# One attention-and-MLP block on one core: last q tile moved, a start-up reordered, and two loads and a broadcast rewritten as 128-row copies

## The chip, the cores and the metric

The kernel runs on one core of a Trainium2 chip. The metric is device time in microseconds (us) of one execution. The kernel before takes 828.01 us, the median of three runs (827.72 to 828.8).

## What is computed

```python
x = A_x                                            # 1 x 2048 x 1024, bf16
mod = (silu(c) @ w_mod).reshape(1, 6, 1, 1024)     # sa, ca, ga, sb, cb, gb
h = layernorm(x) * (1 + ca) + sa
q, k, v = split(h @ wqkv)                          # 32 heads of 32
pq, pk = phi(q), phi(k)                            # phi(t) = (t + 1 if t > 0 else exp(t)) + 1e-6
kv = einsum('bhsd,bhse->bhde', pk, v);  z = sum_s pk
o = (pq @ kv) / (pq . z + 1e-6)
x = x + ga * (o @ wo)
h = layernorm(x) * (1 + cb) + sb
x = x + gb * ((silu(h @ w_gate) * (h @ w_up)) @ w_down)
```

## The kernel before

The program writes one list of instructions for each engine by hand, in the order in which the calls stand; semaphore waits are derived from which bytes an instruction reads and writes. Nothing is reordered later, so an instruction that waits holds back all that stand behind it on its engine. All DMAs but one tiny one are issued from SyncE's queue (SP), in order too. A PSUM bank is taken over by another engine only when the last user of the bank is done.

**Start (lines 597 to 660).** Four row tiles of 128 rows are normalised and transposed on TensorE. Tiles 0 and 2 get mean and variance from VectorE (`s0_`, `s2_`: two bn_stats and an aggregation), tiles 1 and 3 from sums on ScalarE (`act_stats`, `ve_sums`). GpSimd raises the variance to -1/2, VectorE applies it (`ln1_xn`, `ln1_xn_sum`), then TensorE transposes 8 blocks (`tile_transposes`). Between them stand filler matmuls on a tile of zeros (`warm`), whose result nobody reads. `mod_sc` makes columns of the scale 1+ca and of the shift sa with one-column matmuls into bank 0; `fin_ca` and `fin_sa` copy them out; `h0_first` scales the transposed tile.

**q of the first 512 rows (`q_phase_chunk0`, lines 773 to 847).** Seven q tiles stand in seven banks and are summed over the 8 blocks `dt` as weights and scales arrive; bank 0 holds the small products. The effect of the shift on q goes through a bias (`bias_mm`, `bias_fin`, `BIASQ`). The eighth q tile comes last, in bank 0. ScalarE evicts each q tile twice (`q_phi`: Exp and Relu), VectorE combines them (`q_min`, `q_add`).

**k of the first 512 rows, then chunks 1 to 3 (lines 849 to 932).** Each `k_group` or `q_group` is 8 matmuls into the bank that `next_bank` gives. `kside` hangs VectorE work behind the k groups of chunk 0, among it the scaling of chunk 1's transposed rows (`th_mod(1, ...)`).

**The middle (lines 934 to 1073).** Since o @ wo is linear in v, the weights are folded: G = x-hat^T pk in 16 `g_group`s of 16 matmuls in five banks, evicted by `g_evac` (ScalarE and VectorE, one group behind); `kvt_mm` and `m_mm` make the folded weight MW from G, WV and WO, a half at a time. `den` makes the denominators on TensorE, VectorE inverts them, the result goes to DRAM (`recip_den`, 32 heads x 2048 rows) and comes back spread over 128 partitions (RB: each head's row on 32 partitions). `scale_pq(hg)` multiplies the phi of q by RB on VectorE; the `wo_part` matmuls then use it. `wo_load` brings wo into WO; `fold_ga` scales WO by ga on VectorE. The order of this stage is the loop of lines 1038 to 1061:

```python
for g in range(16):
    g_group(g)
    while ev < g + 1 - (3 if g < 4 else 2 if g < 6 else 1):
        g_evac(ev); ev += 1
    ...
    if 6 <= g <= 9:  fold_ga(2 * (g - 6)); fold_ga(2 * (g - 6) + 1)
    if g == 10:      kvt_mm(0)
    if 11 <= g < 13: m_mm(0, g - 11, ...)
    if 7 <= g < 15:  scale_pq(g - 7)
```

After the loop stand `g_evac(15)`, four loads of x, six `wo_part` matmuls, `kvt_mm(1)` and the rest of MW. The load `stgx1` reuses the memory of RB, and the loads of x that of the normalised rows.

**The rest.** Projection and residual, the second normalisation, then the gate, up and down matmuls with streamed weights.

Of the kernel before, what the change touches and what calls it, by code (L numbers as in the profile page):

```python
# [5 lines left out]
FP32 = mybir.dt.float32  # L6
# [256 lines left out]
def bass_adaLN_cond__linear_attn_block__swiglu_ffn__prompt_kernel(  # L263
# [22 lines left out]
    with ExitStack() as es:  # L286
# [6 lines left out]
        def T(name, off, shape, dt):  # L293
            n = 1
            for s_ in shape[1:]:
                n *= s_
            assert off % 32 == 0 and off + n * mybir.dt.size(dt) <= ARENA, (name, off, shape)
            return nc.alloc_sbuf_tensor_at(name, shape, dt, offset=base + off)
# [47 lines left out]
        RL = T("rl", 188 * KB, [128, 4, 512], BF16)  # L346
        E1X = T("e1x", 192 * KB, [128, 4, 512], BF16)
        RLX = T("rlx", 196 * KB, [128, 4, 512], BF16)
        ACC = T("acc", 192 * KB, [128, D], FP32)
        MHL = T("mhl", 196 * KB, [128, 2, D], BF16)  # L350
        MHLT = T("mhlt", 192 * KB, [128, 2 * NDT, 128], BF16)
# [105 lines left out]
        def warm(n=1, bank=2):  # L457
            for _ in range(n):
                P.pe("matmul", out=PS[:, bank, :], lhsT=IDENT[:], rhs=E1[:, 0, :], start=True, stop=True)
# [23 lines left out]
        def ln1_xn(st, c0=0, c1=D):  # L483
            P.dve("tensor_scalar", out=XRES[:, st, c0:c1], in0=XRES[:, st, c0:c1],
                  scalar1=MV[:, st, 0:1], scalar2=RSTD[:, st:st + 1], op0=ALU.subtract, op1=ALU.mult)
# [139 lines left out]
                  op0=ALU.add, op1=ALU.add)  # L625
            pool_pow(st)

        warm(13, bank=3)
        act_stats(1)
        act_stats(3)  # L630
        for f in s0_:
# [1 line left out]
        ln1_rstd1(0)  # L633
        msq_neg(1)
        s2_[0]()
        ln1_xn(0)
        tile_transposes(0)
        warm(5, bank=3)
        ve_sums(1)
        s2_[1]()  # L640
        s2_[2]()
        ln1_rstd1(2)
        ln1_xn_sum(1)
        tile_transposes(1)
        warm(1, bank=3)
        msq_neg(3)
        ln1_xn(2, 0, 512)
        ve_sums(3)
        ln1_xn(2, 512, D)
        tile_transposes(2)  # L650
        mod_sc(WCA, 8, range(2))
        ln1_xn_sum(3, 0, 512)
        ln1_xn_sum(3, 512, D)
        fin_ca(0, 2)
        tile_transposes(3)
        mod_sc(WCA, 8, range(2, 4))
        h0_first(0, "dve")
        h0_first(1, "dve")
        raw_copy(4, "dve")
# [43 lines left out]
        def next_bank():  # L703
            i = qk_ctr[0]
            qk_ctr[0] += 1
            return (1, 2, 3, 4, 6, 7, 5, 0)[i % 8] if i < 40 else i % 5 + 1

        def q_group(ch, nt):
            buf, bank = ch % 2, next_bank()
# [39 lines left out]
        def mod_row_b(bank, i, dst):  # L749
# [3 lines left out]
            P.wait_for("sp", [wr])  # L753
            P.dma("mdr%d" % i, dst[:], MDR[i].unsqueeze(0).to_broadcast([128, D]))

        def q_slot(nt):
            return (E1, RL) if nt < 4 else (E1X, RLX)

        def q_phi(nt, bank):
            for buf, fn_ in zip(q_slot(nt), (ACT.Exp, ACT.Relu)):  # L760
                P.act("activation", out=buf[:, nt % 4, :], in_=PS[:, bank, :], func=fn_, bias=BIASQ[:, nt:nt + 1])

        def q_min(nts):
            for nt in nts:
                e = q_slot(nt)[0][:, nt % 4, :]
                P.dve("tensor_scalar", out=e, in0=e, scalar1=1.0, scalar2=1e-6, op0=ALU.min, op1=ALU.add)

        def q_add(nts):
            for nt in nts:
                e, r = q_slot(nt)  # L770
                P.dve("tensor_tensor", out=PQT[:, nt, 0:512], in0=r[:, nt % 4, :], in1=e[:, nt % 4, :], op=ALU.add)

        def q_phase_chunk0():
            qb = [1, 2, 3, 4, 6, 7, 5]
            fin_ca(2, 2)
            for dt in (2, 3):
                h0_first(dt, "dve")
            for nts, dts in ((range(3), (0,)), (range(3), (1,)), ((3, 4, 5, 6), (0, 1))):
                for nt in nts:
                    q_part(nt, qb[nt], dts)  # L780
            for nt in range(7):
                if nt == 4:
                    mod_sc(WCA, 8, range(4, 8))
                    fin_ca(4, 4)
                    for dt in (4, 5):
                        h0_scale_only(dt)
                q_part(nt, qb[nt], (2, 3))
            act_stats(4, (0,))
            for nt in range(7):
                if nt == 6:  # L790
                    mod_sc(WSA, 0, range(6, 8))
                    fin_sa(6, 2)
                    for dt in (6, 7):
                        h0_scale(dt)
                q_part(nt, qb[nt], (4, 5))
            mod_sc(WSA, 0, range(4, 6))
            fin_sa(4, 2, True)
            for dt in (4, 5):
                h0_shift(dt)
            for nt in range(7):  # L800
                if nt == 2:
                    bias_mm((4, 5))
                q_part(nt, qb[nt], (6,))
            for nt in range(7):
                if nt == 1:
                    mod_sc(WSA, 0, range(4), range(4))
                if nt == 3:
                    mod_sc(WSA, 0, range(4), range(4, 8))
                    fin_sa(0, 4, True)
                    ln_ops[1][0]()  # L810
                if nt == 5:
                    bias_mm(range(4))
                    bias_fin()
                q_part(nt, qb[nt], (7,))
            ln_ops[1][1]()
            ln_ops[1][2]()
            ln1_rstd1(5)
            for i, dt in enumerate((4, 5, 0, 1, 2, 3, 6, 7)):
                P.pe("matmul", out=PS[:, 0, :], lhsT=WQK[:, dt, 896:1024], rhs=HT[:, 0, dt, :], start=(i == 0),
                     stop=(i == 7))  # L820
            for dt in range(4):
                h0_shift(dt)
            ln1_xn(5)
            th_dma(5)
            for nt in range(2):
                q_phi(nt, qb[nt])
            act_stats(4, (1,))
            for nt in range(2, 8):
                q_phi(nt, qb[nt] if nt < 7 else 0)
            for f in ln_ops[2]:  # L830
                f()
            act_var(4)
            pool_pow(4)
            for f in ln_ops[3]:
                f()
            ln1_rstd2(6)
            ln1_xn_sum(4)
            th_dma(4)
            q_min((0, 1))
            for st in (6, 7):  # L840
                ln1_xn(st)
                th_dma(st)
            q_add((0, 1))
            for nts in ((2, 3), (4, 5)):
                q_min(nts)
                q_add(nts)
            qk_ctr[0] = 0

        def add(d, k, f):
            d.setdefault(k, []).append(f)  # L850
# [1 line left out]
        kside = {}  # L852
        ln_ops = [ln1_stats_ops(4 + jj) for jj in range(4)]

        for c0 in (0, 256):
            for dt in range(NDT):
                add(kside, 1, lambda dt=dt, c0=c0: th_mod(1, dt, c0, c0 + 256))
        add(kside, 1, lambda: q_min((6, 7)))
        add(kside, 1, lambda: q_add((6, 7)))
        for jj, k in ((0, 3), (1, 4)):  # L860
            add(kside, k, lambda jj=jj: act_stats(10 + jj))
        q_phase_chunk0()
        for st in range(12, 16):
# [68 lines left out]
        phi_flush()  # L932

        def wo_load(f):
            outs = [WO[32 * g:32 * g + 32, 4 * f:4 * f + 4, :] for g in range(4)]

            def fn(e, outs=outs, f=f):
                return [e.dma_start(out=o_, in_=wov[f, g]) for g, o_ in enumerate(outs)]

            P.add("sp", fn, reads=[], writes=outs, lane="wo%d" % f, ninc=4, tag="wo")  # L940

        G_BANKS = [0] + [next_bank() for _ in range(4)]

# [26 lines left out]
        def den():  # L970
            for hg in range(NHG):
                for ch in range(NCH):
                    P.pe("matmul", out=PS[32 * ch:32 * ch + 32, 7, :], lhsT=ZSEL[:, hg * 32:hg * 32 + 32],
                         rhs=PQT[:, hg, ch * 512:(ch + 1) * 512], start=(hg == 0), stop=(hg == NHG - 1),
                         skip_group_check=True)
            P.dve("tensor_scalar", out=DEN[:], in0=PS[:, 7, :], scalar1=1e-6, scalar2=None, op0=ALU.add)
            P.dve("reciprocal", out=RCP[:], in_=DEN[:])
            P.dve("tensor_copy", out=RCB[:], in_=RCP[:])
            wr = [P.dma("rdr%d" % ch, RDR[:, ch * 512:(ch + 1) * 512], RCB[32 * ch:32 * ch + 32, :])
                  for ch in range(NCH)]  # L980
            P.wait_for("sp", wr)
            for gh in range(2):
                outs = [RB[32 * hh:32 * hh + 32, 4 * gh:4 * gh + 4, :] for hh in range(4)]
                ins = [RDR.rearrange("(g x) s -> x g s", x=4)[hh, 4 * gh:4 * gh + 4].unsqueeze(0).to_broadcast([32, 4, S])
                       for hh in range(4)]

                def fn(e, outs=outs, ins=ins):
                    return [e.dma_start(out=o_, in_=i_) for o_, i_ in zip(outs, ins)]

                P.add("sp", fn, reads=[], writes=outs, lane="rb%d" % gh, ninc=4, tag="rb")  # L990

        def scale_pq(hg):
            P.dve("tensor_tensor", out=PQT[:, hg, :], in0=PQT[:, hg, :], in1=RB[:, hg, :], op=ALU.mult)
# [254 lines left out]
```

## Time and profile before

| what | us |
|---|---|
| median of three runs | 828.01 |
| the profiled execution, its own time | 827.71 |
| span of its instructions | 826.0 |
| VectorE busy in the span | 312.2 (38%) |
| ScalarE busy | 197.0 (24%) |
| GpSimd busy | 41.0 (5%) |
| one 128x512 matmul, start to start | 0.216 |
| one g_group (16 matmuls) | 3.45 |

A matmul's own record is longer (0.379 us) than its pitch of 0.216 us, since matmuls overlap in the array. Times inside the execution count from the first instruction. The 1.7 us between span and own time lie around the program. The stages by the clock of the trace: start to 12 us, q of the first rows to 29 us, k and q of all rows to 126 us, the middle to about 192 us, the projection to about 240 us, the MLP to the end.

### The profile page before, as it was taken

Reading aid. Unit: us, or ns where it says so; the run is one execution under the profiler, and the core shown is the slowest. Engines: PE = TensorE matmul, PEld = TensorE weight load, DVE = VectorE, ACT = ScalarE, POOL = GpSimd, SP = SyncE. Lnnn points to the kernel's source line nnn. Section 1 sums busy time; section 2 is a strip of 40 time slices with the busy share of each in tenths; the row PEclk is TensorE's granted clock in tenths of the full one; section 3 lists DMA queues with packets and bytes.
Section 4 is the critical chain, followed back from the end, with each engine's and each line's share of the span. In section 5 each row is a group of like instructions: output and inputs, shape, how many; then the busy total and the mean of one; then the engine's idle time right before and its main releaser. Section 6 shows DMA issues by size and latency. Waiting matters only on the chain.

```text
span 826.0 us, 10436 instructions
## 1 busy us (share of the span) xinstructions
PE 816.3 (99%) x4243; PEld 375.9 (46%) x4322; DVE 312.2 (38%) x672; ACT 197.0 (24%) x338; POOL 41.0 (5%) x58
## 2 busy tenths in 40 slices
PE   8999999999999999999999999999999999999998
PEld 4544444444444444444444444444444444444444
DVE  5798988477945521111221112122111111221111
ACT  4758642123341111011111101111110111111011
POOL 1110000000130000020000003000000300000000
DMA  9969756865698995600455570045557004553000
GB/s 316 297 139 223 167 159 149 181 175 211 149 253 245 296 249 153 166 26 26 136 151 151 153 174 25 23 131 153 151 152 182 27 19 126 151 152 88 0 26 26
DMA packets 199392, 119.32 MB, mean 144 GB/s; under 512 B 58024, under 2 KB 183088, under 8 KB 199344
## 3 DMA queue, kind: packets, MB, share of 16 engines
q1 hardware_dynamic: 199328, 118.65, 53.8%
q8 instruction: 34, 0.56, 0.3%
q14 instruction: 14, 0.11, 0.0%
q10 hardware_dynamic: 16, 0.00, 0.0%
HBM read 100.67 MB, written 4.33 MB: 127 GB/s over the span
## 4 chain that ended last, share of the span: by engine, by line
PE 98%; issue 1%; DMA 0%; DVE 0%; POOL 0%; SPq 0%
PE ps L176 98%; DMA xres<-in_A_x_dram 0%; POOL rstd L176 0%; DVE xres L176 0%; DVE stats L176 0%; SPq L176 0%; DVE ht L176 0%; DVE ve L176 0%; DVE mv L176 0%; DVE modcol L176 0%
## 5 line engine op out<-in xcount | busy, mean ns | idle before, releaser
L176 PE MATMUL ps<-h2t,gug 128*128 128x512 bf16 x878 | 210.1, 379 | 0.9
L176 PE MATMUL ps<-h2t,guu 128*128 128x512 bf16 x878 | 209.9, 379 | 0.9
L176 DVE TENSOR_TENSOR at<-sg,ps 128x512 bf16<-128x512 bf16 x112 | 77.0, 687 | 282.8 <-PE ps L176 270.6
L176 ACT ACTIVATE sg<-ps 128x512 bf16<-128x512 f32 x112 | 66.9, 597 | 309.7 <-PE ps L176 298.3
L176 PEld LDWEIGHTS ps<-h2t,guu 128*128 128x128 bf16 x896 | 87.7, 98 | 105.7
L176 PEld LDWEIGHTS ps<-h2t,gug 128*128 128x128 bf16 x896 | 87.6, 98 | 105.5
L176 PE MATMUL ps<-wd_a,at 128*128 128x512 bf16 (+1 forms) x502 | 111.9, 377 | 0.5
L176 PE MATMUL ps<-ht,wqk 128*128 128x512 bf16 x499 | 110.7, 379 | 0.9 <-DVE ht L176 0.2
L176 PE MATMUL ps<-wd_b,at 128*128 128x512 bf16 (+1 forms) x377 | 84.6, 377 | 0.4
L176 PEld LDWEIGHTS ps<-wd_a,at 128*128 128x128 bf16 x512 | 50.1, 98 | 59.6
L176 DVE TENSOR_TENSOR ut<-att,gb_b 128x512 bf16<-128x512 bf16 (+1 forms) x32 | 13.6, 426 | 167.5 <-ACT att L176 167.5
L176 PEld LDWEIGHTS ps<-ht,wqk 128*128 128x128 bf16 x512 | 49.2, 98 | 58.9 <-DVE ht L176 1.0
L176 ACT ACTIVATE att<-ps 128x512 bf16<-128x512 f32 (+1 forms) x32 | 17.4, 591 | 182.1 <-PE ps L176 182.1
L176 PEld LDWEIGHTS ps<-wd_b,at 128*128 128x128 bf16 x384 | 37.6, 98 | 44.7
L176 PE MATMUL ps<-pk,xres 128*128 128x512 bf16 x250 | 55.4, 379 | 0.6 <-issue 0.5
L176 PE MATMUL ps<-mw,pqt 128*128 128x512 bf16 x249 | 55.4, 379 | 0.5 <-issue 0.2
L176 POOL TENSOR_SCALAR h2t<-h2t,modcol 128x512 bf16<-128x512 bf16 x32 | 26.5, 846 | 383.0 <-DMA h2t<-xn 383.0
L176 ACT ACTIVATE e<-ps 128x512 bf16<-128x512 f32 x56 | 33.3, 611 | 31.8 <-PE ps L176 15.8
L176 ACT ACTIVATE junk<-xres 128x1024 bf16<-128x1024 bf16 x26 | 27.6, 1063 | 45.9 <-DVE xres L176 34.2
L176 PEld LDWEIGHTS ps<-mw,pqt 128*128 128x128 bf16 x256 | 24.8, 98 | 30.0 <-issue 0.5
L176 PEld LDWEIGHTS ps<-pk,xres 128*128 128x128 bf16 x256 | 24.6, 98 | 30.1 <-issue 1.3
L176 DVE SCALAR_TENSOR_TENSOR xres<-ps,xres 128x512 bf16<-128x512 f32 x32 | 21.5, 688 | 11.6 <-PE ps L176 11.3
(111 smaller groups left out, 337.8 us busy)
## 6 DMA issues: line engine op xcount, KB each, us to landing
gug<-in_B_w_gate_dram SPq DMA_DIRECT2D x56, 512.0 KB, 4.0
guu<-in_B_w_up_dram SPq DMA_DIRECT2D x56, 512.0 KB, 5.3
xres<-in_A_x_dram SPq DMA_DIRECT2D x20, 256.0 KB, 4.4
rb<-recip_den SPq DMA_DIRECT2D x8, 512.0 KB, 11.7
stgx<-in_w_mod_dram SPq DMA_DIRECT2D x2, 2048.0 KB, 9.3
wd_a<-in_B_w_down_dram SPq DMA_DIRECT2D x4, 1024.0 KB, 7.7
out_dram<-xres SPq DMA_DIRECT2D x31, 128.0 KB, 1.7
xres<-in_A_x_dram SPq DMA_DIRECT2D x3, 1024.0 KB, 6.5
```

The lines of the kernel that those rows point to most:

```text
L176: return getattr(e, method)(**kw)
```

## The change

- **Start:** 14 instead of 13 fillers ahead of the first transposes, then 1 and 2 in place of 5 and 1. Tile 2's second bn_stats, tile 1's variance and tile 2's aggregation stand ahead of tile 0's normalisation on VectorE. The scale columns are made 3 and 1 tiles at a time in place of 2 and 2.
- **q of the first rows:** the first q tile is copied out raw (`QRAW`, one more ScalarE instruction), and the eighth q tile takes its bank instead of bank 0. The eighth tile's matmuls stand around the shift and bias products. Both passes of tile 4's statistics stand together, the q tiles are finished in the order 1 to 7, then 0, and the bank order of the k groups follows.
- **Side work of chunk 0's k:** th_mod of blocks 4 to 7 goes at full width (12 instructions in place of 16), the last four q tiles are combined behind the fourth k group, and two statistics move one group later.
- **DMAs of the middle:** `wo_load`, the write of the reciprocals and their broadcast RB get another form; sizes and count of loads (8 of 256 KB, 8 of 512 KB) stay, the write is one of 128 KB in place of four of 32 KB. RB now has a semaphore for each of its 8 blocks in place of one for 4 blocks.

In the built program the leading counts of the access patterns are, DRAM side first:

| copy | before | after |
|---|---|---|
| wo | 32 x 4 x 1024 to 32 partitions x 4 x 1024 | 4 x 32 x 1024 to 128 partitions x 1024 |
| recip_den, written | 32 x 512 from 32 partitions | 4 x 32 x 512 from 128 partitions |
| recip_den, read into RB | 32 (step 0) x 4 x 2048 to 32 partitions x 4 x 2048 | 4 x 32 (step 0) x 2048 to 128 partitions x 2048 |

```diff
-        warm(13, bank=3)
+        warm(14, bank=3)
...
         s2_[0]()
+        s2_[1]()
+        ve_sums(1)
+        s2_[2]()
+        ln1_rstd1(2)
         ln1_xn(0)
         tile_transposes(0)
-        warm(5, bank=3)
-        ve_sums(1)
-        s2_[1]()
-        s2_[2]()
-        ln1_rstd1(2)
+        warm(1, bank=3)
         ln1_xn_sum(1)
         tile_transposes(1)
-        warm(1, bank=3)
+        warm(2, bank=3)
...
-        mod_sc(WCA, 8, range(2))
+        mod_sc(WCA, 8, range(3))
...
-        fin_ca(0, 2)
+        fin_ca(0, 3)
         tile_transposes(3)
-        mod_sc(WCA, 8, range(2, 4))
+        mod_sc(WCA, 8, range(3, 4))
...
             for nt in range(7):
-                if nt == 1:
+                q_part(nt, qb[nt], (7,))
+                if nt == 0:
+                    P.act("activation", out=QRAW[:], in_=PS[:, qb[0], :], func=ACT.Copy)
+                    act_stats(4)
+            for i, dt in enumerate(range(NDT)):
+                if i == 1:
                     mod_sc(WSA, 0, range(4), range(4))
-                if nt == 3:
+                if i == 3:
                     mod_sc(WSA, 0, range(4), range(4, 8))
+                    ln_ops[1][0]()
                     fin_sa(0, 4, True)
...
+                P.pe("matmul", out=PS[:, qb[0], :], lhsT=WQK[:, dt, 896:1024], rhs=HT[:, 0, dt, :], start=(i == 0),
+                     stop=(i == 7))
...
-        for c0 in (0, 256):
-            for dt in range(NDT):
-                add(kside, 1, lambda dt=dt, c0=c0: th_mod(1, dt, c0, c0 + 256))
-        add(kside, 1, lambda: q_min((6, 7)))
-        add(kside, 1, lambda: q_add((6, 7)))
+        for dt, c0, c1 in ([(dt, 0, 256) for dt in range(4)] + [(dt, 256, 512) for dt in range(4)]
+                           + [(dt, 0, 512) for dt in range(4, 8)]):
+            add(kside, 1, lambda dt=dt, c0=c0, c1=c1: th_mod(1, dt, c0, c1))
+        for i in (4, 6):
+            add(kside, 3, lambda i=i: q_pair(i))
...
         def wo_load(f):
-            outs = [WO[32 * g:32 * g + 32, 4 * f:4 * f + 4, :] for g in range(4)]
+            outs = [WO[:, 4 * f + h, :] for h in range(4)]
...
-                return [e.dma_start(out=o_, in_=wov[f, g]) for g, o_ in enumerate(outs)]
+                return [e.dma_start(out=o_, in_=wov[f, :, :, h, :]) for h, o_ in enumerate(outs)]
...
-            wr = [P.dma("rdr%d" % ch, RDR[:, ch * 512:(ch + 1) * 512], RCB[32 * ch:32 * ch + 32, :])
-                  for ch in range(NCH)]
-            P.wait_for("sp", wr)
-            for gh in range(2):
-                outs = [RB[32 * hh:32 * hh + 32, 4 * gh:4 * gh + 4, :] for hh in range(4)]
...
+            wr = P.dma("rdr", RDR.rearrange("h (c s) -> c h s", c=NCH), RCB[:])
+            P.wait_for("sp", [wr])
+            for hg in range(NHG):
+                rb_ = RB[:, hg, :]
+                rows = RDR[4 * hg:4 * hg + 4, :].unsqueeze(1).to_broadcast([4, 32, S])
```

More of the change, by code (lines that the diff above doesn't have):

```diff
@@ L348, in bass_adaLN_cond__linear_attn_block__swiglu_ffn__prompt_kernel @@
         RLX = T("rlx", 196 * KB, [128, 4, 512], BF16)
+        QRAW = T("qraw", 202 * KB, [128, 512], FP32)
         ACC = T("acc", 192 * KB, [128, D], FP32)
@@ L705, in next_bank @@
             qk_ctr[0] += 1
-            return (1, 2, 3, 4, 6, 7, 5, 0)[i % 8] if i < 40 else i % 5 + 1
+            if i < 24:
+                return (0, 2, 3, 4, 6, 7, 5, 1)[i % 8]
+            if i < 40:
+                return (0, 2, 3, 4, 6, 1, 7, 5, 0, 2, 3, 1, 4, 6, 7, 5)[i - 24]
+            return i % 5 + 1
         def q_group(ch, nt):
@@ L754, in mod_row_b, with q_phi @@
             P.dma("mdr%d" % i, dst[:], MDR[i].unsqueeze(0).to_broadcast([128, D]))
+        QORD = (1, 2, 3, 4, 5, 6, 7, 0)
         def q_slot(nt):
-            return (E1, RL) if nt < 4 else (E1X, RLX)
-        def q_phi(nt, bank):
+            i = QORD.index(nt)
+            bufs = (E1, RL) if i < 4 else (E1X, RLX)
+            return [t[:, i % 4, :] for t in bufs]
+        def q_phi(nt, src):
             for buf, fn_ in zip(q_slot(nt), (ACT.Exp, ACT.Relu)):
-                P.act("activation", out=buf[:, nt % 4, :], in_=PS[:, bank, :], func=fn_, bias=BIASQ[:, nt:nt + 1])
+                P.act("activation", out=buf, in_=src, func=fn_, bias=BIASQ[:, nt:nt + 1])
         def q_min(nts):
             for nt in nts:
-                e = q_slot(nt)[0][:, nt % 4, :]
+                e = q_slot(nt)[0]
                 P.dve("tensor_scalar", out=e, in0=e, scalar1=1.0, scalar2=1e-6, op0=ALU.min, op1=ALU.add)
@@ L770, in q_add, with q_pair @@
                 e, r = q_slot(nt)
-                P.dve("tensor_tensor", out=PQT[:, nt, 0:512], in0=r[:, nt % 4, :], in1=e[:, nt % 4, :], op=ALU.add)
+                P.dve("tensor_tensor", out=PQT[:, nt, 0:512], in0=r, in1=e, op=ALU.add)
+        def q_pair(i):
+            q_min(QORD[i:i + 2])
+            q_add(QORD[i:i + 2])
         def q_phase_chunk0():
             qb = [1, 2, 3, 4, 6, 7, 5]
-            fin_ca(2, 2)
+            fin_ca(3, 1)
             for dt in (2, 3):
@@ L787, in q_phase_chunk0 @@
                 q_part(nt, qb[nt], (2, 3))
-            act_stats(4, (0,))
             for nt in range(7):
@@ L804, in q_phase_chunk0 @@
             for nt in range(7):
-                if nt == 1:
+                q_part(nt, qb[nt], (7,))
[4 more added lines that the diff above has]
+                if i == 1:
                     mod_sc(WSA, 0, range(4), range(4))
-                if nt == 3:
+                if i == 3:
                     mod_sc(WSA, 0, range(4), range(4, 8))
+                    ln_ops[1][0]()
                     fin_sa(0, 4, True)
-                    ln_ops[1][0]()
-                if nt == 5:
+                    ln_ops[1][1]()
+                    act_var(4)
+                    pool_pow(4)
+                if i == 5:
                     bias_mm(range(4))
                     bias_fin()
-                q_part(nt, qb[nt], (7,))
-            ln_ops[1][1]()
+                P.pe("matmul", out=PS[:, qb[0], :], lhsT=WQK[:, dt, 896:1024], rhs=HT[:, 0, dt, :], start=(i == 0),
+                     stop=(i == 7))
             ln_ops[1][2]()
             ln1_rstd1(5)
-            for i, dt in enumerate((4, 5, 0, 1, 2, 3, 6, 7)):
-                P.pe("matmul", out=PS[:, 0, :], lhsT=WQK[:, dt, 896:1024], rhs=HT[:, 0, dt, :], start=(i == 0),
-                     stop=(i == 7))
             for dt in range(4):
                 h0_shift(dt)
+            ln1_xn_sum(4)
+            th_dma(4)
             ln1_xn(5)
             th_dma(5)
[L825 to L829, printed above, removed]
+            for nt in QORD:
+                q_phi(nt, QRAW[:] if nt == 0 else PS[:, qb[nt % 7], :])
             for f in ln_ops[2]:
                 f()
-            act_var(4)
-            pool_pow(4)
             for f in ln_ops[3]:
@@ L836, in q_phase_chunk0 @@
             ln1_rstd2(6)
-            ln1_xn_sum(4)
-            th_dma(4)
-            q_min((0, 1))
+            q_min(QORD[0:2])
             for st in (6, 7):
@@ L842, in q_phase_chunk0 @@
                 th_dma(st)
[L843 to L846, printed above, removed]
+            q_add(QORD[0:2])
+            q_pair(2)
             qk_ctr[0] = 0
@@ L853, in bass_adaLN_cond__linear_attn_block__swiglu_ffn__prompt_kernel @@
         ln_ops = [ln1_stats_ops(4 + jj) for jj in range(4)]
-        for c0 in (0, 256):
-            for dt in range(NDT):
-                add(kside, 1, lambda dt=dt, c0=c0: th_mod(1, dt, c0, c0 + 256))
-        add(kside, 1, lambda: q_min((6, 7)))
-        add(kside, 1, lambda: q_add((6, 7)))
-        for jj, k in ((0, 3), (1, 4)):
+        for dt, c0, c1 in ([(dt, 0, 256) for dt in range(4)] + [(dt, 256, 512) for dt in range(4)]
[3 more added lines that the diff above has]
+            add(kside, 3, lambda i=i: q_pair(i))
+        for jj, k in ((0, 4), (1, 5)):
             add(kside, k, lambda jj=jj: act_stats(10 + jj))
@@ L934, in wo_load @@
         def wo_load(f):
-            outs = [WO[32 * g:32 * g + 32, 4 * f:4 * f + 4, :] for g in range(4)]
+            outs = [WO[:, 4 * f + h, :] for h in range(4)]
             def fn(e, outs=outs, f=f):
-                return [e.dma_start(out=o_, in_=wov[f, g]) for g, o_ in enumerate(outs)]
-            P.add("sp", fn, reads=[], writes=outs, lane="wo%d" % f, ninc=4, tag="wo")
+                return [e.dma_start(out=o_, in_=wov[f, :, :, h, :]) for h, o_ in enumerate(outs)]
+            P.add("sp", fn, reads=[], writes=[WO[:, 4 * f:4 * f + 4, :]], lane="wo%d" % f, ninc=4, tag="wo")
         G_BANKS = [0] + [next_bank() for _ in range(4)]
@@ L978, in den, with fn @@
             P.dve("tensor_copy", out=RCB[:], in_=RCP[:])
-            wr = [P.dma("rdr%d" % ch, RDR[:, ch * 512:(ch + 1) * 512], RCB[32 * ch:32 * ch + 32, :])
-                  for ch in range(NCH)]
-            P.wait_for("sp", wr)
-            for gh in range(2):
-                outs = [RB[32 * hh:32 * hh + 32, 4 * gh:4 * gh + 4, :] for hh in range(4)]
[L984 to L990, printed above, removed]
+            wr = P.dma("rdr", RDR.rearrange("h (c s) -> c h s", c=NCH), RCB[:])
[3 more added lines that the diff above has]
+                rows = RDR[4 * hg:4 * hg + 4, :].unsqueeze(1).to_broadcast([4, 32, S])
+                def fn(e, rb_=rb_, rows=rows):
+                    return [e.dma_start(out=rb_, in_=rows)]
+                P.add("sp", fn, reads=[], writes=[RB[:, hg, :]], lane="rb%d" % hg, tag="rb")
         def scale_pq(hg):
```

## The prediction

> **What bounds the kernel now.** The busy row comes first, then what PE waited for (columns: us, times, mean us), then the middle cut into windows.
>
> ```profile
> PE 816.3 (99%) x4243; PEld 375.9 (46%) x4322; DVE 312.2 (38%) x672; ACT 197.0 (24%) x338; POOL 41.0 (5%) x58
> ```
>
> ```profile
> PE ps L176 <- DMA cs<-in_c_dram: 2.2, 1, 2.2
> PE ps L176 <- issue: 0.6, 4, 0.2
> PE ps L176 <- DVE e L176: 0.2, 1, 0.2
> PE ps L176 <- DVE ht L176: 0.2, 1, 0.2
> ```
>
> PE sets the time. The 2.2 us lie ahead of the first filler, the 0.2 on `e` is the filler's zeros. All other waits of PE sum to 0.8 us, and between dense matmuls I find only four gaps of the reordered parts (22.4, 26.1, 44.4 and 46.4 us: 0.09, 0.06, 0.04, 0.13). Whatever the edits of the first 60 us do, they can win about half a us; what they can lose is open. So the question is what new wait PE meets, and the place to look is where transfers change form.
>
> ```profile
> 137.00:147.00 10.00, 9.95 (x47) 4.55 (x47) 7.53 (x8) 4.47 (x7) 0.00 (x0) 1.00 1.00 226
> 151.00:161.00 10.00, 9.95 (x47) 4.58 (x47) 2.13 (x4) 0.72 (x1) 0.00 (x0) 1.00 0.99 218
> 161.00:170.00 9.00, 8.84 (x165) 4.53 (x164) 8.72 (x12) 1.45 (x2) 0.00 (x0) 1.00 1.00 205
> 173.00:177.00 4.00, 3.84 (x33) 1.62 (x32) 3.10 (x6) 1.72 (x4) 0.00 (x0) 1.00 1.05 400
> ```
>
> Columns: length, busy of PE, PEld, DVE, ACT, POOL, granted clock, busy DMA engines (1.00 is all 16), GB/s. Row one is wo, rows two and three RB: all 16 engines busy, at 226, 218 and 205 GB/s, 12.8 to 14.1 per engine. Row four is x, loaded as 128 rows: 400, or 23.8 per engine (16.8 by the share).
>
> ```profile
> 161.28 1.22 DVE L176 TENSOR_TENSOR pqt<-pqt,rb 128x2048 bf16<-128x2048 bf16 x1 [6.65 <-DMA rb<-recip_den]
> 166.39 1.28 PE L176 MATMUL ps<-g,wv 128*32 128x32 bf16 x128
> 187.26 1.19 PE L176 MATMUL ps<-g,wv 128*32 128x32 bf16 x128
> ```
>
> These are `scale_pq(0)`, `kvt_mm(0)` and `kvt_mm(1)` (start, length, in brackets the idle time before). VectorE already stands 6.65 us in order behind the first half of RB (landed 161.25, the second 170.98), and PE does not feel it yet.
>
> **The change, part by part.** *Start.* Dense work now begins near 11.8 us. The chain to it is x landed 6.61, tile 3's sums 8.97, variance 9.30, GpSimd 9.59 to 10.24, normalised 10.27, transposes 10.74, `h0_first` 11.14. None of it is removed; tile 2's 1.2 us of bn_stats go ahead of tile 0's normalisation, which takes VectorE work from the later path and delays transposes(0) from 6.98 to about 8.0, with filler 14 ending near 7.13 (start plus 14 at the pitches shown by the first 13: eight at 0.427, then 0.216). The clock was warm after eight fillers, each 0.211 longer than later ones; if the 0.85 us of idleness cooled it again, 7 x 0.211 = 1.5 us are lost. I take a gain of 0.2 (bounds: 0.3 won, 1.5 lost): no wait of that length after warming stands in this trace. Scale columns 3+1 instead of 2+2 are the same 64 small matmuls.
>
> *q and k of the first rows.* Added: one ScalarE copy of 128x512, priced by the like eviction at 0.61; ScalarE is busy 3.17 of 15.2 us from 12 to 27.2, and six matmuls (1.3 us) pass before its bank is written again. Without cover it costs at most 0.6. The eighth tile's 8 matmuls are moved, not added. What changes is the gaps above: 0.2 won of 0.32. The four fewer th_mod instructions and later q adds ease VectorE at 44 to 60 us (15.75 of 16 busy). Were that to pile up instead, I bound it by two half-width instructions, 1 us. Start and q together: -0.4 (bounds -0.6 to +3.1, both losses and an uncovered copy).
>
> *wo, reciprocals, RB.* Bytes are equal: 2.097 MB, 0.131 MB, 4.194 MB. The SP queue issues them in the old order, the write with one instruction for four, the RB copies eight as before; nothing is moved past another queue. What differs is the leading count, now 4 in DRAM against 128 in SBUF. In this trace the count tells how many engines serve a copy: the semaphores of the copies with 8 leading rows (c and the two modulation rows) rise in 9 steps, those with 32 or 128 rows in 16 steps. All have one count on both sides, so 4 against 128 is not shown. I take the smaller to divide the copy: four engines of 16. The other bound is all 16, priced below.
>
> [...]
>
> The price per engine has two ends: 12.8 to 14.1 (32-row rows above, all engines into a quarter of the partitions) and 23.8 (128 rows). The destination is now 128 rows of 2 or 4 KB, as in the row of x, so I take 23.8. No row shows a lone engine.
>
> - wo: 524,288 B for each of four engines / 23.8 = 22.0 us. At 226 GB/s wo took 9.3 and ended at 147.9 (last issue 138.3, longest landing 9.6), so it began at 138.6, and now ends at 160.6. Its first half lands near 149.6, when `fold_ga(0)` wants it (149.9).
> - Reciprocals: 32,768 B, 1.4 us, behind wo on the same four engines: 162.0 (before: 149.2).
> - RB: before, its first half landed 12.0 us after the issue at 149.3, of which 2.097 MB at 218 GB/s are 9.6; 2.4 are start-up. Now 131,072 B each, 5.5 us: the first lands at 162.0 + 2.4 + 5.5 = 169.9, the eighth at 164.4 + 44.1 = 208.5.
>
> What is late next: `scale_pq(g-7)` stands in VectorE's list after each group, and it holds back `g_evac` behind it, the copy of KVT, and so PE. `kvt_mm(0)` needs the eviction of group 7, behind `scale_pq(0)`: it starts late once RB's first block lands after about 164. Group 14 needs a bank evicted behind `scale_pq(4)`. `kvt_mm(1)` needs the eviction of group 15, behind `scale_pq(7)`: that is the last wait, and the earlier ones lie inside it. After RB's last block come 1.21 (scale) and two evictions, 2.6 us with what stands between, then the 0.44 from eviction to `kvt_mm(1)` (186.82 to 187.26): 211.5, against 187.26. **+24.2 us.** The loads of x queue behind RB on the same engines: `stgx1` needs `scale_pq(3)` and took 9 us, the next are wanted later in the projection, which moves too; I count nothing (bound: 2 us).
>
> Before `kvt_mm(1)`, PE has stood for several us; the clock warms again, as in the first fillers: +1.5.
>
> **Sum.** Span 826.0 - 0.4 + 24.2 + 1.5 = 851.3. Around the span lay 1.7 (own time 827.71), and the median of the runs is 0.3 above it: +2.0, so **853 us**.
>
> **Rivals.**
> - *Half rate.* [...] By 13.8 per engine wo takes 38.0 (176.6), the write 2.4 (179.0), RB 2.4 + 8 x 9.5 (257.4), `kvt_mm(1)` comes at 257.4 + 3.0 = 260.4, +73.2; 902 us. With 12.8 per engine wo takes 41.0 and RB 81.9, 911. For: every copy here that leaves most partitions out ran at that rate with all engines busy. [...]
>
> [...]
>
> - *All 16 engines (not slower).* The copies are divided by their 128 SBUF rows, or by descriptors. RB then lands by 400 GB/s in 10.5 us, earlier than before, which PE does not feel: the 6.65 us of VectorE go, PE was at 9.95 of 10. The time is 828.0 - 0.4 = 827.6. It decides wherever RB's first block lands before 164 and one follows each 3.45 us (a group). For: the loop's order still places one scaling per group from group 7 on, fitting blocks that land apart. Against: the 9 steps.
> - *The start cools the clock*, with 16 engines: 828.0 + 1.5 - 0.2 = 829.3. For: 0.85 us without a matmul; against: clock rows show 1.00 throughout once warm.
>
> **How the numbers follow.** Four engines at full rate 0.36 (own range 850 to 874: 1.606 MB per engine take 67.5 us at 23.8, 64.2 at 400/16 = 25, 85.4 at 18.8, midway to the half rate; the 3.1 of the start on top), half rate 0.30, all 16 engines 0.28 (0.03 of it with a gain over 0.2%), start or VectorE slower 0.06 (half over 0.2%). About 0.2%, 1.7 us, is what a measurement tells from no change. Slower: 0.36 + 0.30 + 0.03 = 0.69; same 0.25 + 0.03 = 0.28; faster 0.03. The range reaches from 827 (16 engines) to 906, midway between the half rate's 902 and 911.
>
> **What would show it.** Right: DMA share near 0.25 at about 95 GB/s from 139 to 208, eight waits of VectorE on `rb` of some us each, PE waiting on `g` before `kvt_mm(0)`, in group 14 and before `kvt_mm(1)` at about 211, where the granted clock falls. At 55 GB/s to 257 the half rate is right. Start: transposes(0) at about 8.0, dense work near 11.6, one `qraw` copy on ScalarE, and no gaps at 44 to 47. Wrong: RB's first block by 160 and no wait of PE, a share of 1.00 in that stage, or a loss that lies ahead of 130 us.

## The result, and the profile after

The changed kernel takes 855.65 us (median of five, 854.07 to 857.12), the kernel before 828.01 us in the same comparison: a ratio of 1.033, 95% interval 1.0313 to 1.0347. The execution in the profile took 854.07, its span is 852.3, 26.3 us more than before.

First the busy row of the page, then the chain that ended last, by engine.

```profile
PE 821.3 (96%) x4241; PEld 377.2 (44%) x4320; DVE 312.3 (37%) x668; ACT 197.8 (23%) x339; POOL 40.8 (5%) x58
...
PE 82%; DMA 7%; SPq 3%; DVE 3%; ACT 3%; issue 1%; POOL 0%; ACTq 0%; DVEq 0%
```

The chain was 98% PE before and now has 7% of DMA in it. What PE waited for (us, times, longest):

```profile
PE ps L176 <- DVE g L176: 16.0, 2, 13.7
PE ps L176 <- DVE kvt L176: 4.0, 1, 4.0
PE ps L176 <- DMA cs<-in_c_dram: 2.8, 1, 2.8
PE ps L176 <- issue: 1.0, 5, 0.3
PE ps L176 <- DVE ht L176: 0.6, 2, 0.4
PE ps L176 <- ACT ht L176: 0.4, 1, 0.4
```

Twenty us are new waits for VectorE's evictions. They name VectorE, but VectorE was itself waiting. Its timeline has the eight `scale_pq`; six of them are shown, without the other work (start, length, in brackets the idle time before):

```profile
167.59 1.23 DVE L176 TENSOR_TENSOR pqt<-pqt,rb 128x2048 bf16<-128x2048 bf16 x1 [12.43 <-DMA rb<-recip_den]
...
172.61 1.23 DVE L176 TENSOR_TENSOR pqt<-pqt,rb 128x2048 bf16<-128x2048 bf16 x1 [1.93 <-DMA rb<-recip_den]
...
187.69 1.23 DVE L176 TENSOR_TENSOR pqt<-pqt,rb 128x2048 bf16<-128x2048 bf16 x1 [1.92 <-DMA rb<-recip_den]
...
193.67 1.22 DVE L176 TENSOR_TENSOR pqt<-pqt,rb 128x2048 bf16<-128x2048 bf16 x1 [2.89 <-DMA rb<-recip_den]
...
201.94 1.23 DVE L176 TENSOR_TENSOR pqt<-pqt,rb 128x2048 bf16<-128x2048 bf16 x1 [6.39 <-DMA rb<-recip_den]
...
208.47 1.23 DVE L176 TENSOR_TENSOR pqt<-pqt,rb 128x2048 bf16<-128x2048 bf16 x1 [4.65 <-DMA rb<-recip_den]
```

All eight end a wait for RB, 35.1 us in all; before, the one wait of this kind was 6.65. Up to the fifth, a block comes each 5.03 us (in the trace's semaphores they land at 167.56 to 187.67); the last three take 6.0, 8.3 and 6.5 us, and the eighth lands at 208.45. PE's timeline shows where that is felt, with `kvt_mm(0)`, the first `m_mm`, the first projection matmuls and `kvt_mm(1)`:

```profile
169.62 0.96 PE L176 MATMUL ps<-g,wv 128*32 128x32 bf16 x100 [2.33 <-DVE g L176]
...
179.81 0.44 PE L176 MATMUL ps<-wo,kvt 32*32 32x512 bf16 x16 [3.99 <-DVE kvt L176]
...
210.42 1.03 PE L176 MATMUL ps<-mw,pqt 128*128 128x512 bf16 x2 [13.70 <-DVE g L176]
...
213.09 1.23 PE L176 MATMUL ps<-g,wv 128*32 128x32 bf16 x128
```

The windows of this stage (length, busy of PE, PEld, DVE, ACT, POOL, granted clock, DMA share, GB/s):

```profile
150.00:160.00 10.00, 9.95 (x47) 4.56 (x47) 3.66 (x6) 1.44 (x2) 0.00 (x0) 1.00 0.25 97
...
170.00:180.00 10.00, 5.86 (x98) 2.52 (x90) 5.85 (x9) 1.02 (x2) 0.00 (x0) 0.83 0.26 106
180.00:190.00 10.00, 9.83 (x65) 3.80 (x51) 5.39 (x7) 3.71 (x7) 0.00 (x0) 0.83 0.26 106
190.00:200.00 10.00, 6.72 (x32) 2.84 (x29) 2.67 (x4) 1.12 (x2) 0.00 (x0) 1.00 0.97 219
200.00:210.00 10.00, 0.00 (x0) 0.00 (x0) 3.41 (x4) 0.72 (x1) 0.00 (x0) 0.58 0.59 169
210.00:220.00 10.00, 8.98 (x183) 4.01 (x187) 4.54 (x10) 2.17 (x4) 0.00 (x0) 0.73 0.14 54
```

A share of 0.25 is four engines of 16, and 106 GB/s by 0.26 x 16 engines are 25.5 GB/s for each; before, RB ran at a share of 0.99 to 1.00 with 218 and 205 GB/s. The semaphores say the same in the trace: each of the eight RB copies is counted up in 5 steps, one lump at the issue and four engines. At 190 the share jumps to 0.97 and RB gets slower: there the load `stgx1`, issued at 184.65, runs on the other twelve. The last column but two is the second finding: the granted clock is below 1.00 after each of these waits of PE (0.83, 0.83 and 0.73), and within the longest.

### The profile page after: what moved, and what is told of

It reads as the page before. It is cut to its first block, busy times and chain, and to the rows that moved or that the text cites. A ratio compares the mean times of both kernels' runs of the same rounds, so it can differ in the third digit from the quotient of the medians.

```text
span 852.3 us, 10425 instructions
## 1 busy us (share of the span) xinstructions
PE 821.3 (96%) x4241; PEld 377.2 (44%) x4320; DVE 312.3 (37%) x668; ACT 197.8 (23%) x339; POOL 40.8 (5%) x58
## 4 chain that ended last, share of the span: by engine, by line
PE 82%; DMA 7%; SPq 3%; DVE 3%; ACT 3%; issue 1%; POOL 0%; ACTq 0%; DVEq 0%
PE ps L176 82%; DMA rb<-recip_den 4%; SPq L176 2%; DMA recip_den<-rcb 2%; SPq L996 2%; DMA xres<-in_A_x_dram 1%; DVE pkt L176 1%; ACT e L176 1%; ACT rl L176 1%; ACT junk L176 1%; DVE ht L176 0%; DMA ht<-xres 0%; DVE e L176 0%; DVE acc L176 0%; ACT ht L176 0%
## 5 line engine op out<-in xcount | busy, mean ns | idle before, releaser
L176 PE MATMUL ps<-mw,pqt 128*128 128x512 bf16 x249 | 56.9, 386 | 14.5 <-DVE g L176 13.7
L176 PE MATMUL ps<-pk,xres 128*128 128x512 bf16 x250 | 58.8, 395 | 0.6 <-issue 0.5
```

The source lines that it names most:

```text
L176: return getattr(e, method)(**kw)
```

## The experiments

Each experiment gives its median and, in brackets, its ratio to the kernel before with the 95% interval. The kernel before, measured beside them, took 828.00 us for the first two sections and the first try on the gaps, 827.89 for the three sections between, and 828.15 for the last two runs.

### Taking the copies back

```diff
-            outs = [WO[:, 4 * f + h, :] for h in range(4)]
+            outs = [WO[32 * g:32 * g + 32, 4 * f:4 * f + 4, :] for g in range(4)]
...
-            wr = P.dma("rdr", RDR.rearrange("h (c s) -> c h s", c=NCH), RCB[:])
+            wr = [P.dma("rdr%d" % ch, RDR[:, ch * 512:(ch + 1) * 512], RCB[32 * ch:32 * ch + 32, :])
+                  for ch in range(NCH)]
...
-                rows = RDR[4 * hg:4 * hg + 4, :].unsqueeze(1).to_broadcast([4, 32, S])
+                outs = [RB[32 * hh:32 * hh + 32, 4 * gh:4 * gh + 4, :] for hh in range(4)]
...
```

> The changed kernel with the three copies (wo, reciprocals, RB) in the form of before; all else as changed. Theory (the copies with a leading count of 4 make the whole loss): the loss of 27.6 us is gone, all copies of the stage show 16 increments of their semaphores per copy, kvt_mm(1) comes within 1 us of 187.3, and the time is 827.5 to 829.0. Within it, the gap that the changed kernel shows at 71.5 us (0.8 us, q or k matmuls that wait for the shifted rows of chunk 2) stays, so that the time is rather 828.3 than 827.6. Rival (the reordering of the first 60 us carries part of the loss): 830 or more.

Measured: 828.34 us against 828.00 (1.0005, 0.9996 to 1.0013); RB arrives early enough again, and PE has no wait over 0.3 us after 12 us. `kvt_mm(1)` comes 0.55 us later than in the kernel before:

```profile
187.81 1.20 PE L176 MATMUL ps<-g,wv 128*32 128x32 bf16 x128
```

The three copies make the whole loss, as far as it stands out from the noise. The small gaps stay, as was said: behind the matmuls at 71.7 and 72.6 the next one starts 0.48 and 0.26 us later than the pitch of 0.216.

### Each copy by itself

RB alone, in the kernel before:

```diff
-            for gh in range(2):
-                outs = [RB[32 * hh:32 * hh + 32, 4 * gh:4 * gh + 4, :] for hh in range(4)]
...
+            for hg in range(NHG):
+                rb_ = RB[:, hg, :]
+                rows = RDR[4 * hg:4 * hg + 4, :].unsqueeze(1).to_broadcast([4, 32, S])
...
```

> The kernel before with RB's read alone in the changed form (8 copies of 4 rows by 32, a semaphore each); wo, the write of the reciprocals and the start as before. Theory (4 engines, 26 GB/s each as the changed kernel showed): reciprocals in DRAM at 149.2 as before, first block 7.5 us later at 156.7, then one each 5.05 us until the load of stgx1 collides with the last three; the eighth at 192 without and 198 with that collision. kvt_mm(0) is on time (no wait at 166), group 14 and the bank for the first projection matmuls wait; kvt_mm(1) at 197 to 202.5; time 838 to 844. Rival (wo is what makes RB late, RB's own copies are hidden): 829 or less.

Measured: 844.02 us (1.0191, 1.0177 to 1.0205), at the upper edge of 838 to 844. `kvt_mm(0)` is on time (166.87, no wait), RB's blocks are used at 157.87, 162.90, 167.91 and so on each 5.0 us, then the last three at 6.2, 8.1 and 6.4 us: the slow end of the changed kernel again. PE has one wait:

```profile
200.43 2.74 PE L176 MATMUL ps<-mw,pqt 128*128 128x512 bf16 x6 [13.49 <-DVE g L176]
```

And wo alone, in the kernel before:

```diff
-            outs = [WO[32 * g:32 * g + 32, 4 * f:4 * f + 4, :] for g in range(4)]
+            outs = [WO[:, 4 * f + h, :] for h in range(4)]
...
```

> The kernel before with the loads of wo alone in the changed form. Theory (4 engines): wo's second half lands near 158.8 instead of 147.8; the write of the reciprocals goes through all 16 engines, but its share on those four stands behind wo, so that it ends near 159.5 and RB's first half lands near 171.5 (before 161.25), the second near 181. kvt_mm(0) waits some 7 us at 166.5, one cold restart of the clock of 1.7 us follows, and nothing else waits long: time 836 to 839. Rival (wo's lateness costs nothing by itself, since fold_ga has slack): 828 to 829.

Measured: 838.04 us (1.0119, 1.0103 to 1.0134). The loads of wo end at 159.5, the write of the reciprocals, in its old form over 16 engines, at 160.2; the semaphore of each of its four copies shows twelve engines done at 152 to 154 and four at 158 to 160. RB's first half lands at 172.06, 10.8 us later than before. VectorE waits for it, and PE has one long wait, at `kvt_mm(0)`:

```profile
172.08 1.23 DVE L176 TENSOR_TENSOR pqt<-pqt,rb 128x2048 bf16<-128x2048 bf16 x1 [17.43 <-DMA rb<-recip_den]
...
174.12 0.99 PE L176 MATMUL ps<-g,wv 128*32 128x32 bf16 x100 [7.34 <-DVE g L176]
```

This is how a transfer that nobody waits for costs time: `fold_ga` had slack, what stood behind wo on its four engines had none. The two parts, 16.0 and 10.0 us, sum to 26.0 of the 27.6. That they nearly add is chance in part, as we read it: wo's lateness stalls PE at 166, RB's slow arrival at 187. The new form of the write was not tried alone; behind wo it ended at 160.1 in the new form (the changed kernel) and at 160.2 in the old (here).

### Is it the leading count that sets the engines?

```diff
-                rb_ = RB[:, hg, :]
-                rows = RDR[4 * hg:4 * hg + 4, :].unsqueeze(1).to_broadcast([4, 32, S])
+                rb_ = [RB[64 * i:64 * i + 64, hg, :] for i in range(2)]
+                rows = [RDR[4 * hg + 2 * i:4 * hg + 2 * i + 2, :].unsqueeze(1).to_broadcast([2, 32, S]) for i in range(2)]
...
```

> The changed kernel with each block of RB read by two copies of 2 rows by 32 into 64 partitions, in place of one of 4 rows by 32 into 128; bytes, rows and bytes per row as in the changed kernel. Theory (the smaller leading count sets the number of engines, and copies of the same count use the same engines): each copy shows 3 increments of its semaphore, two engines carry everything, a block takes 10.1 us, the DMA share of the stage is near 0.13, the eighth block lands at 243 to 249, kvt_mm(1) comes near 250, time 890 to 898. Rival (the engines are given by rows, one for each 32, or two copies take different engines): four engines again, a block each 5 us, time 853 to 858.

Measured: 893.27 us (1.079, 1.0769 to 1.0812). Each copy is counted up in three steps, both copies of a block use the same two engines one after the other (a block's halves land 5.0 us apart), and a block takes 10.0 us. A window of that kernel in which RB runs alone, columns as above:

```profile
175.00:185.00 10.00, 5.90 (x115) 2.82 (x116) 3.09 (x5) 0.73 (x2) 0.00 (x0) 0.78 0.13 54
```

0.13 of 16 are two engines; 54 GB/s are 26 for each. The bytes, the rows in all and the length of a row are unchanged; each copy has half the rows. What halved is the leading count, and with it the engines. The rival (engines by the place of a group of 32 rows, or two copies on different engines) would have stayed at four. One engine for each 32 rows of a copy would also give two, but the load `stgx1` has 128 rows and is counted in 16 steps. In none of the changed copies is the smaller count on the SBUF side, so whether the smaller count decides or the one on the DRAM side is not told apart.

### Why RB's last blocks were slow

`rbs` are the eight copies of RB; the loads now wait until the last of them has landed.

```diff
...
-            if g == 10:
-                P.dma("stgx1", STGX[0][:], wmv[:, :, 3072:4096])
         g_evac(15)
+        P.wait_for("sp", rbs[7:])
         for st in range(4):
             P.dma("xr%d" % st, XRES[:, st, :], xv[:, st, :])
+        P.dma("stgx1", STGX[0][:], wmv[:, :, 3072:4096])
```

> The changed kernel with the loads of x and of stgx1 held back until RB's last block has landed (in the changed kernel stgx1 is issued at 184.65 and the blocks of RB that land after 190 take 6.0, 8.3 and 6.5 us in place of 5.05). Theory (those loads, on the 12 engines that are free, slow the four that carry RB): all blocks at 5.05, the eighth at 203 instead of 208.4, kvt_mm(1) 5.5 us earlier, time 849.5 to 852 unless x is then late. Rival (the last blocks are slow for another reason, such as a full queue): the eighth block at 208 again, time 855 or more.

Measured: 849.73 us (1.026, 1.0243 to 1.0277), 5.9 below the changed kernel. In its profile the last three blocks keep the distance of the others, 5.0 us each:

```profile
192.01 1.22 DVE L176 TENSOR_TENSOR pqt<-pqt,rb 128x2048 bf16<-128x2048 bf16 x1 [1.91 <-DMA rb<-recip_den]
...
197.00 1.22 DVE L176 TENSOR_TENSOR pqt<-pqt,rb 128x2048 bf16<-128x2048 bf16 x1 [1.91 <-DMA rb<-recip_den]
...
202.00 1.23 DVE L176 TENSOR_TENSOR pqt<-pqt,rb 128x2048 bf16<-128x2048 bf16 x1 [3.11 <-DMA rb<-recip_den]
...
206.97 1.23 DVE L176 TENSOR_TENSOR pqt<-pqt,rb 128x2048 bf16<-128x2048 bf16 x1 [3.09 <-DMA rb<-recip_den]
```

So a load on twelve idle engines is not free for the four that carry RB: beside it their 4 KB packets took 284 ns in the mean between 192 and 200, where it was 160 between 165 and 190. The loads slowed as well: 2 KB packets took 150 ns between 192 and 200, and 85 between 173 and 177 in the kernel before, where `stgx1` ran alone. What makes each slower beside the other was not tried. (This execution, at 852.88 the longest of four, stands 2.6 us late from its first stage on, for a reason told below, and RB's first block 4.5 us; only distances are read from it.)

### What a cold clock costs

```diff
+        for _ in range(62):
+            P.pe("matmul", out=PS[:, 7, :], lhsT=IDENT[:], rhs=WV[:, 0, 0:512], start=True, stop=True)
         wo_part(0, 0, range(4))
```

> The changed kernel with 62 matmuls more, whose result nobody reads, behind the last g_group, where PE waits 13.7 us (they take 62 x 0.216 = 13.4 us). Theory (the idle time cools the clock, and the matmuls after the wait run at 0.427 instead of 0.216 for some 8 or 9 matmuls): the granted clock stays at 1.00 from 186 to 220, and the time is 1.2 to 2.0 us below the changed kernel's, near 854. Rival (the slow matmuls come from something else than idleness, or the wait is set so that PE's speed after it doesn't matter): within 0.5 of the changed kernel, or slower.

Measured: 853.16 us (1.0305, 1.0289 to 1.032), 2.5 below the changed kernel's median; the two were measured in different comparisons, whose kernels before stand 0.1 apart, and the intervals overlap. So the 2.5, more than the 1.2 to 2.0 expected, is not a firm size. The windows bear the mechanism out:

```profile
196.00:210.00 14.00, 13.89 (x64) 6.27 (x64) 3.77 (x5) 0.90 (x2) 0.00 (x0) 1.00 0.71 187
210.00:220.00 10.00, 9.79 (x196) 4.65 (x197) 6.12 (x16) 2.95 (x5) 0.00 (x0) 1.00 0.14 53
```

The granted clock of 210 to 220 is 1.00, it was 0.73; with useless matmuls in the wait, the useful ones after it run at full pace. Inside the two executions, the stretch from the first projection matmul to the one behind the last `m_mm` takes 5.62 us (210.06 to 215.68) instead of 7.45 (210.42 to 217.87), 1.8 less.

### The gaps at 71.5 us

The reordered start lost something too, too small to matter beside the copies: chunk 2's first matmuls wait 0.5 and 0.3 us for their scaled rows. The first guess was the two statistics that move one k group later.

```diff
-        for jj, k in ((0, 4), (1, 5)):
+        for jj, k in ((0, 3), (1, 4)):
```

> As the run before it, and the two statistics of tiles 10 and 11 hang behind the third and fourth k group again, as before, in place of the fourth and fifth. Theory (the later statistics keep ScalarE busy when it should scale chunk 2's rows, and so make the 0.8 us at 71.5): no gap over 0.1 us between 70 and 75, time 0.6 to 0.8 below the run beside it, near 827.5. Rival (the gap comes from the fewer, wider th_mod steps or the new bank order): the gap stays, and the two times agree within 0.3.

Measured: 828.47 us against 828.34 without it, and the gaps stay (0.48 and 0.26). The guess was wrong. VectorE's timeline of the first experiment shows an idle stretch ahead of the k groups that the kernel before hasn't (there it combines q tiles up to 38.4):

```profile
39.09 0.29 DVE L176 TENSOR_SCALAR e<-e 128x512 bf16<-128x512 bf16 x1 [1.17 <-ACT e L176]
```

Behind that stretch, both pairs that were put off (1.07 us each) are done at 46 to 48, and from there on each of its instructions is 0.9 us later than before, the evictions of ScalarE behind it too, up to the rows that PE waits for at 71.7.

```diff
             q_pair(2)
+            q_pair(4)
             qk_ctr[0] = 0
...
-        for i in (4, 6):
+        for i in (6,):
             add(kside, 3, lambda i=i: q_pair(i))
```

> forms_back (the changed kernel with the copies of before), and the pair of q tiles 5 and 6 is combined on VectorE ahead of the k groups, as before, in place of behind the fourth k group. The statistics' place turned out not to make the gap at 71.5 us. New theory: VectorE stood idle for 1.17 us at 37.9 in that kernel, and the 2.1 us of the two pairs went into a stretch (44 to 62 us) in which it is never idle, so that all that follows comes 0.9 us late up to chunk 2's rows. With one pair (1.07 us) back in the idle stretch, the gaps at 71.6 and 72.6 (0.48 and 0.26 us) fall under 0.2 in sum, and the time is 0.5 to 0.8 us below forms_back, 827.5 to 827.8. Rival (ScalarE, which finishes the q tiles 0.9 us later than before, is what is late): the gaps stay, and both agree within 0.3.

> forms_back once more, beside the run above and on its chip. All theories: 828.1 to 828.6, with the gaps at 71.6 and 72.6 in the trace.

Measured beside each other: 827.41 us with the pair moved, 828.65 without: 1.2 apart, where 0.5 to 0.8 was expected. In the first both gaps are gone; in the second they stay, so the place of the pairs made them. Against the kernel before the first is 0.9993 (0.9984 to 1.0002): the best median of all versions here, but not told apart from before.

The second's profiled execution took 830.7, the longest of its eleven, and shows one thing more. Its window from 12 to 16 us, columns as above, and that of the same program in the first experiment:

```profile
12.00:16.00 4.00, 3.87 (x21) 1.62 (x20) 2.25 (x6) 2.52 (x3) 0.00 (x0) 0.58 1.08 361
```

```profile
12.00:16.00 4.00, 4.00 (x20) 1.84 (x19) 1.50 (x5) 2.06 (x3) 0.00 (x0) 1.00 1.08 360
```

In the longer one the fourth tile of x landed at 7.70 instead of 6.53. ScalarE waited 1.27 us for it, VectorE, in order behind ScalarE's sums, normalised the third tile's second half later, and PE waited 0.79 us in the middle of the third tile's transposes. The dense matmuls began at 12.56 instead of 11.81, and from 12.60 on the clock was at half for 3.41 us: seven of their first nine steps took 0.427 instead of 0.216, the other two 0.37 and 0.27, 1.7 us in all. The profiled execution with late loads shows the same from 13.2 us on. These two are, of the eight profiled executions with the reordered start, those with the latest fourth tile (7.70 and 7.21; the others 6.38 to 6.71). What the old order would have done with x as late was not tried.

## Why the prediction was right, step by step

**The deciding step, four engines, held.** It was the smaller of the two leading counts, and the author's choice: the copies with 9 and 16 semaphore steps have one count on both sides. The runs show 5 steps for a count of 4 and 3 for a count of 2, with the engines' share to match (0.25 to 0.26, and 0.13).

**The rate.** Forecast 23.8 GB/s per engine, by a row that the forecast calls x. It is not x: the one load in flight from 173 to 177 us is `stgx1` (issued at 170.57, landed at 177.96 to 179.53), and x is issued from 182.83 on. `stgx1` too goes to 128 rows, so the price stands. Measured were 26.1 (131,072 B in 5.03 us) for RB and 25.6 for wo (262,144 B in the 10.26 us between its halves). So the half-rate rival (13.8) fell: the price by rows of 32 partitions does not carry over to four engines into 128. wo landed at 158.8 (forecast 160.6), the reciprocals at 160.1 (162.0), the first block at 167.56 (169.9).

**RB's end was right by two errors that cancel.** The eighth block landed at 208.45, the forecast was 208.5. At 5.03 us a block it would have been 202.8; the collision with `stgx1` and the loads of x gave 5.7 us back, where the step on these loads counted nothing and bounded 2 us. The loads were expected to queue behind RB on its engines. They did, in their share on those four (`stgx1` at 212.4 to 213.4); their other twelve engines did not wait (200.5 to 201.5), and slowed RB. Taking them away gained 5.9 us. So it is partly luck that 853 lies only 2.7 us from the measured 855.65: the mechanism was right, and the sizes of its parts were off in both directions.

**The last wait** was expected at `kvt_mm(1)`. It fell on the six projection matmuls ahead of it, whose bank the eviction of group 14 frees; they then ran cold, and `kvt_mm(1)` came at 213.09 instead of 211.5. The forecast missed these six: at full clock they cost 1.3 us, and in the kernel before they do not wait.

**Waits and clock traded places.** The forecast had 24.2 us of delay and one cold restart of 1.5. The trace has 20.0 us of waits (2.3, 4.0 and 13.7) and three restarts, since the clock is at half from 170.96, 181.2 and 201.68 on; PE's busy time rose by 5.0 us. Of the waits named in advance, the one in group 14 did not come; the 4.0 are the first `m_mm`, which waits for the copy of KVT behind the third scaling. With 0.8 for the gaps at 71.5 and 0.3 for a later first filler that makes 26.1 of the 26.3.

**The start and q.** Forecast -0.4. Alone it measured +0.3 and +0.5 (1.0005, within the noise, and 1.001): the gaps at 44 and 46 us are gone, but the put-off pairs cost 0.7 to 0.8 at 71.5. What was won ahead of that would be 0.1 to 0.3 (`kvt_mm(0)` comes 0.6 later in the first experiment and 0.5 in the changed kernel, less those gaps). This is not shown: in the kernel with RB alone, whose start is unchanged, `kvt_mm(0)` comes 0.5 later too. The forecast's sentence that later q adds ease VectorE failed; the bound beside it, 1 us if they pile up, was the right one. The rival of the cold start came in two of the eight profiled executions, and by another wait than the one it named: 0.73 us without a matmul ahead of the first transposes left the clock at 1.00 in the first experiment.

## What to carry to other kernels

Read the leading count on both sides of every copy, and count the steps of its semaphore: a form that looks better, one copy to all 128 partitions, can put four engines to work where the copy to 32 partitions used 16 (here a share of 0.26 in place of 0.99). A transfer's lateness can be charged where the next thing on its engines is waited for (here that of wo, as a wait of 7.34 us of PE, behind VectorE's for RB), so follow both the bytes behind it and the instructions that stand in order behind its consumer. And where TensorE stops, look at the granted clock from there on, and add its restart to the wait: here 3.41 us at half clock followed a wait of 2.33 us.

## What the runs showed of the hardware

Four engines carried 26.1 GB/s each, two 26, where in the kernel before sixteen came to 23.8 each into 128 partitions (`stgx1`) and to 13.8 in copies to 32 partitions (RB). Neither copy came down to 13.8 on four engines: RB's four counts came in two pairs 0.47 us apart in the changed kernel, about three of its packets of 160 ns; wo's four came 0.1 us after one another at 25.6 GB/s.

The clock's records stood at half speed for 3.41 us, or a multiple of it, at a time (the last one of a run, which its end cuts off, aside): in the changed kernel 3.41 from 170.96, 3.41 from 181.2 and 13.65 from 201.68, in the kernel with wo alone 10.24. How long a wait cools the clock is not settled by these runs. In two executions of one program waits of nearly one length, 0.73 and 0.79 us, went different ways, and the work around the two differs. The first of these rows (first experiment) is followed by full clock, the second (the longer execution) by half from 12.60 on:

```profile
8.09 0.62 PE L176 MATMUL ps<-ident,xres 128*128 128x128 bf16 x8 [0.73 <-DVE xres L176]
```

```profile
10.68 0.40 PE L176 MATMUL ps<-ident,xres 128*128 128x128 bf16 x4 [0.79 <-DVE xres L176]
```

In the changed kernel the clock was at half from 170.96 on, behind a wait of 2.33 us with small matmuls on either side of it.
